# Half-height last products for neighbouring first layer tiles of a gated MLP behind a recurrent attention

## The chip, the cores and the metric

The kernel runs on one core of one Trainium2 chip. The metric is the device time of one execution in microseconds; three executions of the kernel before took 619.6, 621.16 and 621.56 us, so the median is 621.16 us.

## What is computed

The first half is a recurrence over 768 time steps for 4 x 8 heads with a 40 x 40 state, whose output is laid out as `x` of shape 4 x 768 x 320. The second half, which the change touches, is a gated MLP on `x`:

```python
def _moe_ref(x, w_in, g_ln, w_sg, b_sg, w_out):
    h = x @ w_in                        # 320 -> 1024
    h = gelu(h)                         # tanh form
    u, v = h[..., :512], h[..., 512:]
    v_n = layernorm(v) * g_ln           # over the 512
    v_s = einsum('ts,bsd->btd', w_sg, v_n) + b_sg    # over the 768 time steps
    return x + (u * v_s) @ w_out        # 512 -> 320
```

All inputs are float32, and the result has to be near float32: each factor of a product is split into a high and a low part that TensorE's one-pass type (float32r) holds, and a product is taken as high x high + high x low + low x high.

## The kernel before

The recurrence is done by chunks of 64 steps, with all of its products in plain float32. Its last chunks overlap with the first pieces of the MLP; from about 375 us on the MLP is alone. The MLP works on one batch at a time, in pieces whose order is written out in the lists `SEQ0` (batch 0, with the first tiles of batch 1), `SEQ` (batches 1 and 2, each with the tiles of the next) and `SEQL` (batch 3). Each piece is one method of `Mlp`:

- `x0`, `x1` (`split_x`): split 384 time steps of `x` into high `xh` and low `xl`, one ScalarE copy and one VectorE subtraction per block of 128 rows. `x` has 320 rows: two blocks of 128 and one of 64. The third block of `xh` holds the 64 rows twice: the high part in partitions 0 to 63, the low part in 64 to 127. The third block of the weights (`wih`, `wil`) holds the same 64 rows of `w_in` in both halves.
- `v0` to `v5` (`in_v`): 128 time steps by 512 columns of the first layer's `v` half; `u0` to `u7` (`in_u`): 128 columns by 384 time steps of its `u` half. These are the first layer tiles. Each takes eight products into one PSUM bank: `xh` by `wih` (three blocks), `xh` by `wil` (three blocks), `xl` by `wih` (two blocks).
- `s0` to `s7` (`sgu`): 18 products of the spatial layer, from the split `v` tiles and the split spatial weights `wsh`, `wsl`; `o0` to `o5` (`outp`): the second layer, twelve products, or eight for the last 64 rows, which alternate between 64 and 128 columns.

`product` issues a piece's matmuls and hands its later steps to `later`, each with a lag in pieces and a rank; `tick`, called once per piece, issues the steps that are due, in order of rank, and that is the order in which ScalarE, VectorE and GpSimd run them. For a tile these are: lag 0, Square on ScalarE (tile `p`) and the first VectorE step (`q`); lag 1, Tanh on ScalarE (in place in `q`) and the VectorE step that reads the PSUM bank last (into `u` or `v`); for a `v` tile also the norm's statistics (`bs`, `mv`, `rs`), a GpSimd power on `rs`, and with lag 2 the normalisation and the split into `vh` (ScalarE) and `vl` (GpSimd). Every engine runs its instructions in program order. PSUM has eight banks in a ring, one for each piece that multiplies.

Loads and weight splits are `jobs` in `run`, issued ahead of the piece whose place in the sequence they name. The tiles x0, v0, v1, v2, u0 of batch 0 (`FILL`) are issued while the recurrence still runs. `EARLY` is the number of `v` pairs (`vh`, `vl`, 4 KB per partition each pair) that lie in the pool that opens early; the rest lie in the pool that opens after the recurrence.

In the profile nearly all instructions carry line 157, that of the helper that records them, so the rows are read by tiles: `hv` and `hu` are the PSUM tiles of v and u, `sg` and `op` those of the spatial and the second layer, `ab`, `ut`, `pq`, `yp`, `ru` and `sp` belong to the recurrence, `idle` are products without use.

Of the kernel before, what the change touches and what calls it, by code (L numbers as in the profile page):

```python
# [9 lines left out]
F32 = mybir.dt.float32  # L10
F32R = mybir.dt.float32r
I32 = mybir.dt.int32
AF = mybir.ActivationFunctionType
ALU = mybir.AluOpType
PSUM = bass.MemoryType.PSUM

B, H, S, D = 4, 8, 768, 40
# [65 lines left out]
FILL = (("x0", 0, 319.86), ("v0", 0, 331.35), ("v1", 0, 344.98), ("v2", 0, 346.14), ("u0", 0, 349.9))  # L83
AFTER = {"v": (0.56, 0.57, 1.47, 1.57, 2.13, 2.48, 2.96, 4.17, 5.19), "u": (1.14, 1.97, 2.82, 3.17), "x": ()}
PX1 = 0
EARLY = 4
PSG = 313.1
SGD = (-6.74, -0.32, 1.37)
SGA = ()
VRING = 10  # L90
SEQ = ("x0", "s1", "x1", "s2", "s0", "s3", "s4", "v0", "s5", "v1", "o0", "o1", "o2", "s6", "s7", "v2", "u0", "v3",
    "u1", "v4", "v5", "o3", "o5", "o4", "u2", "u3", "u4", "u5", "u7", "u6")
SEQ0 = (("x0", 0), ("v0", 0), ("v1", 0), ("v2", 0), ("u0", 0), ("u3", 0), ("x1", 0), ("u1", 0), ("u2", 0), ("v3",
# [8 lines left out]
XE = "VVVVVVVVVVVV"  # L102
# [23 lines left out]
class Banks:  # L126


    def __init__(self, tc, ctx):
        self.tc, self.ctx, self.n = tc, ctx, 0  # L130
        self.rings = [ctx.enter_context(tc.tile_pool(name="ps", bufs=6, space=PSUM))] * 6
# [30 lines left out]
def engines(tc):  # L162
    nc = tc.nc
    return tuple(InOrder(tc, e) for e in (nc.vector, nc.scalar, nc.gpsimd, nc.tensor, nc.sync))
# [720 lines left out]
class Mlp:  # L885
# [3 lines left out]
    def __init__(self, tc, ps, xd, w_in, w2, g_ln, wst, b_sg, w_out, out):  # L889
        self.tc, self.ps, self.xd, self.out = tc, ps, xd, out  # L890
        self.w_in, self.w2, self.g_ln, self.wst, self.b_sg, self.w_out = w_in, w2, g_ln, wst, b_sg, w_out
        self.V, self.A, self.G, self.T, self.Q = engines(tc)
        self.ctx = ExitStack()
        self.vn, self.us, self.gs, self.xin, self.left, self.outs = {}, {}, {}, {}, [8] * B, {}
        self.ready = set()
        self.n, self.todo, self.plan, self.hold, self.held = 0, [], None, None, {}

    def pool(self, nm, side):
        return self.ctx.enter_context(self.tc.tile_pool(name=nm, bufs=1, side=side, reuse_waits="tile"))
# [8 lines left out]
    def open_x(self):  # L908
        p = self.pool("mlp_x", "right")
        self.xts = {(0, 0): self.xtile(p, 0, 0)}  # L910
        self.xh = p.tile([128, 3, S], F32R, name="xh")
        self.xl = p.tile([128, 2, S], F32R, name="xl")

    def xtile(self, p, b, n):
        return p.tile([128, 3, S // 2], F32, name=f"xt{b}{n}")

    def open_v(self):
        self.pv = p = self.pool("mlp_v", "right")
        self.xts.update({x: self.xtile(p, *x) for x in ((1, 0), (0, 1))})
        self.free = self.pairs(p, 0, EARLY)  # L920
        self.ut = {(f, 0): p.tile([128, 384], F32, name=f"u{f}") for f in range(4)}
# [27 lines left out]
    def open_rest(self):  # L949
# [5 lines left out]
        self.xts[1, 1] = self.xtile(p, 1, 1)  # L955
        self.free += self.pairs(p, EARLY, VRING)
        self.ut.update({(f, 1): p.tile([128, 384], F32, name=f"u{4 + f}") for f in range(4)})
# [126 lines left out]
    def split_x(self, b, n):  # L1084
        t, h, l = self.xts[b % 2, n], self.xh, self.xl
        self.xin[n] = b
        c = slice(384 * n, 384 * n + 384)
        for k in range(2):
            self.split(h[:, k, c], l[:, k, c], t[:, k], self.A, self.pick(XE, 6 * b + 3 * n + k))
        self.A.copy(out=h[:, 2, c], in_=t[:, 2])  # L1090
        self.pick(XE, 6 * b + 3 * n + 2).tensor_tensor(out=h[64:128, 2, c], in0=t[64:128, 2], in1=h[64:128, 2, c].bitcast(F32), op=ALU.subtract)

    def pick(self, s, k):
        return self.G if k < len(s) and s[k] == "G" else self.V

    def product(self, ops, *steps):
        for i, (o, l, r) in enumerate(ops):
            self.T.matmul(o, lhsT=l, rhs=r, start=(i == 0), stop=(i == len(ops) - 1), skip_group_check=True)
        if self.hold is not None:
            self.hold += [f for _, _, f in sorted(steps, key=lambda x: x[:2])]  # L1100
            return
        self.later(*steps)
        self.tick()
# [10 lines left out]
    def in_v(self, b, tt):  # L1114
        V, G, sb = self.V, self.G, self.pv
        xh, xl, wih, wil = self.xh, self.xl, self.wih, self.wil
        c, f = slice(128 * tt, 128 * tt + 128), slice(HF, DF)
        ops = [(xh[:, k, c], x[:, k, f]) for x in (wih, wil) for k in range(3)]
        ops += [(xl[:, k, c], wih[:, k, f]) for k in (0, 1)]
        o, v = self.ps("hv"), sb.tile([128, HF], F32, name="v", bufs=3)  # L1120
        mv = sb.tile([128, 2], F32, name="mv", bufs=3)
        rs = sb.tile([128, 1], F32, name="rs", bufs=3)
        bs = sb.tile([128, 6], F32, name="bs", bufs=3)
        pair = self.free.pop(0)
        assert self.xin[tt // 3] == b

        def root():
            V.tensor_scalar(out=rs, in0=mv[:, 1:2], scalar1=4e-6, scalar2=None, op0=ALU.add)
            G.tensor_tensor(out=rs, in0=rs, in1=self.mhalf, op=ALU.pow)

        def halves():
            h, l = pair
            self.split(h, l, v)
            self.vn[b, tt] = h, l

        self.product([(o, *x) for x in ops], *self.gelu2(o, HF, v),
                     (1, 7, lambda: V.bn_stats(out=bs, in_=v)), (1, 8, lambda: V.bn_aggr(out=mv, in_=bs)), (1, 9, root),
                     (2, 7.5, lambda: V.tensor_scalar(out=v, in0=v, scalar1=mv[:, 0:1], scalar2=rs,
                                                    op0=ALU.subtract, op1=ALU.mult)),
                     (2, 10, halves))  # L1140

    def in_u(self, b, f, n):
        xh, xl, wih, wil = self.xh, self.xl, self.wih, self.wil
        fc, c = slice(128 * f, 128 * f + 128), slice(384 * n, 384 * n + 384)
        ops = [(x[:, k, fc], xh[:, k, c]) for x in (wih, wil) for k in range(3)]
        ops += [(wih[:, k, fc], xl[:, k, c]) for k in range(2)]
        o = self.ps("hu")[:, 0:384]
        assert self.xin[n] == b
        u = self.us[b, f, n] = self.ut.pop((f, n))
        self.product([(o, *x) for x in ops], *self.gelu2(o, 384, u))  # L1150

    def sgu(self, b, f, n):
        V, sb = self.V, self.pr
# [127 lines left out]
    def run(self, ahead, verdict=None):  # L1281

        done = [(x, b) for x, b, _ in FILL] if ahead else []
        seq, jobs = [], []
        if not ahead:
            self.ps.grow()
            self.open_in()
            for g in self.weights_in():
                for f in g(self.G):
                    f()  # L1290
            self.open_x()
            self.open_v()
            self.open_sg()
        self.open_rest()
        for b in range(B):
            seq += [(x, b + (x[0] in "uvx")) for x in (SEQL if b == B - 1 else SEQ)] if b else list(SEQ0)
        seq = [x for x in seq if x[1] < B and x not in done and (ahead or x[0][0] != "j")]
        for i, (x, b) in enumerate(seq):
            if x[0] == "x" and (b or not ahead) and not (ahead and (x, b) == ("x0", 1) and PX1):
                jobs.append((max(0, i - XL), lambda b=b, n=int(x[1]): self.load_x(b, n)))  # L1300
            if verdict and (x, b) == ("s7", 1):
                jobs.append((i, lambda: self.later((8, 9, verdict()))))
        rest, loads, parts, wo = self.weights_rest([(i % 6, i // 6) for i, _ in SGA] if ahead else [])
        jobs += [(REST - 3, rest[0]), (REST, rest[1])]
        for k, f in enumerate(loads):
            if f:
                jobs.append((SGS[k - 5] if k > 4 else 0, f))
        for k, f in enumerate(parts):
            if f:
                jobs.append((SGS[k], f))  # L1310
        for k, g in enumerate(wo):
            for d, f in zip(OSTEP, g):
                jobs.append((OUTS[k] + d, f))
        jobs.sort(key=lambda x: x[0])
        for i, (x, b) in enumerate(seq):
            while jobs and jobs[0][0] <= i:
                jobs.pop(0)[1]()
            self.piece(x, b)
        self.flush()
        self.ctx.close()  # L1320
# [111 lines left out]
```

## Time and profile before

| | before |
|---|---|
| median of three runs | 621.16 us |
| the profiled execution's own time | 620.27 us |
| span of the profiled execution | 618.5 us |
| mean granted TensorE clock | 0.945 |
| TensorE busy | 578.4 us, 94% |
| VectorE busy | 487.2 us, 79% |
| ScalarE busy | 390.9 us, 63% |
| GpSimd busy | 374.3 us, 61% |

Busy time is the time in which an engine has at least one instruction running; loads of TensorE's stationary operand are counted apart (PEld). The ends of products are modelled, and successive products overlap in the record: the time a product takes in a stream is the distance between starts. Span is from the first to the last instruction; the execution's own time has a little more around it.

### The profile page before, as it was taken

To read this page: it belongs to the slowest core of one execution; us is meant where nothing else is said; L and a number is where in the kernel's file an instruction comes from. 1 tells how busy PE (TensorE), PEld (TensorE's weight loads), DVE (VectorE), ACT (ScalarE), POOL (GpSimd) and SP (SyncE) were. 2 spreads that over 40 slices of the span, in tenths; PEclk is the share of its full clock that TensorE was granted. 3 is DMA by queue.
4 is the path that set the end of the run, shared out by engine and by line. 5 is a ranking of instruction groups with operands and counts; after the bars stand their busy time and mean duration, and the time that the engine had idled before them with its cause. 6 is when DMAs were issued, how large, how long until landed. Compare 5 with 4: busy or idle time off the path is not lost.

```text
span 618.5 us, 24511 instructions
## 1 busy us (share of the span) xinstructions
PE 578.4 (94%) x10060; PEld 520.8 (84%) x10060; DVE 487.2 (79%) x1085; ACT 390.9 (63%) x1113; POOL 374.3 (61%) x842
## 2 busy tenths in 40 slices
PE   5758999999999999999979999699999999999996
PEld 5557888888888888888868789699899989999995
DVE  7867798988889897798787988898887779568732
ACT  6938798988979889788764856544544256224410
POOL 7768688888888888888886425445533332343230
PEclk9555899999999999999989999899999999999999
DMA  6513243454434543433433424420111103010002
GB/s 207 168 41 89 76 123 104 121 129 117 113 106 117 132 120 104 116 100 92 140 92 100 129 78 141 141 65 10 33 55 54 34 1 108 1 34 13 20 1 70
DMA packets 56889, 54.06 MB, mean 87 GB/s; under 512 B 35840, under 2 KB 47360, under 8 KB 56768
## 3 DMA queue, kind: packets, MB, share of 16 engines
q1 hardware_dynamic: 56768, 52.40, 29.9%
q8 instruction: 81, 1.33, 0.9%
q14 instruction: 40, 0.33, 0.2%
HBM read 44.52 MB, written 7.86 MB: 85 GB/s over the span
## 4 chain that ended last, share of the span: by engine, by line
PE 50%; DVE 15%; ACT 14%; POOL 9%; issue 6%; DMA 4%; SPq 1%; POOLq 0%; ACTq 0%; DVEq 0%
PE sg L157 13%; PE op L157 6%; PE hu L157 6%; PE hv L157 6%; POOL x L157 5%; POOL tg L157 4%; PE ab L157 4%; ACT nts L157 3%; PE sp L157 3%; PE yp L157 3%; PE ru L157 2%; DVE at L157 2%; DMA main<-main 2%; DVE sc L157 2%; DVE ex L157 2%
## 5 line engine op out<-in xcount | busy, mean ns | idle before, releaser
L157 POOL TENSOR_TENSOR tg<-x,n 128x126 f32<-128x126 f32 (+24 forms) x334 | 123.1, 369 | 34.2 <-ACT x L157 5.5
L157 POOL TENSOR_TENSOR x<-x,tg 128x126 f32<-128x126 f32 (+24 forms) x334 | 126.3, 378 | 26.1
L157 PE MATMUL sg<-wsh,vh 128*128 128x384 f32 x192 | 66.0, 344 | 5.7 <-ACT wsh L157 4.5
L157 POOL TENSOR_TENSOR gx<-g,gy 128x384 fp32r<-128x384 f32 x30 | 31.7, 1061 | 64.6 <-ACT gy L157 64.6
L157 PE MATMUL sg<-wsl,vh 128*128 128x384 f32 x192 | 65.7, 342 | 0.4 <-POOL wsl L157 0.4
L157 PE MATMUL sg<-wsh,vl 128*128 128x384 f32 x192 | 65.7, 342 | 0.0
L157 ACT ACTIVATE nts<-ab 32x256 f32<-32x256 f32 x192 | 62.0, 323 | 5.7 <-DVE at L157 3.1
L157 PE MATMUL pq<-rt,vut 128*64 128x128 f32 x768 | 52.9, 281 | 0.0
L157 ACT CAST gy<-g 128x384 fp32r<-128x384 f32 x30 | 15.4, 514 | 55.5 <-DVE g L157 52.2
L157 PE MATMUL ab<-at,kb 64*64 64x64 f32 x1536 | 38.5, 242 | 11.0 <-POOL kb L157 5.4
L157 ACT CAST vh<-v 128x512 fp32r<-128x512 f32 x24 | 14.9, 621 | 51.6 <-DVE v L157 51.6
L157 PE MATMUL yp<-pqs,kbt 128*64 128x64 f32 x768 | 46.5, 225 | 1.0 <-ACT kbt L157 0.4
L157 PEld LDWEIGHTS ab<-at,kb 64*64 64x64 f32 x1536 | 31.7, 150 | 16.6 <-POOL kb L157 6.0
L157 POOL TENSOR_TENSOR vl<-v,vh 128x512 fp32r<-128x512 f32 x24 | 31.6, 1317 | 20.9 <-ACT vh L157 20.9
L157 PEld LDWEIGHTS pq<-rt,vut 128*64 128x64 f32 x768 | 41.8, 139 | 2.3 <-issue 0.7
L157 PEld LDWEIGHTS sg<-wsh,vh 128*128 128x128 f32 x192 | 36.9, 192 | 6.6 <-ACT wsh L157 4.8
L157 PE MATMUL yp<-rt,s 80*40 80x64 f32 x704 | 42.3, 219 | 0.0
L157 PEld LDWEIGHTS yp<-pqs,kbt 128*64 128x64 f32 x768 | 37.1, 136 | 5.4 <-DVE sc L157 2.2
L157 DVE SCALAR_TENSOR_TENSOR g<-sg,gl,bt 128x384 f32<-128x384 f32 x32 | 19.7, 615 | 25.4 <-PE sg L157 24.4
L157 DVE TENSOR_TENSOR at<-ab,mask 64x256 f32<-64x256 f32 x96 | 35.7, 407 | 4.5 <-PE ab L157 3.9
L157 PEld LDWEIGHTS sg<-wsl,vh 128*128 128x128 f32 x192 | 36.9, 192 | 1.0 <-POOL wsl L157 0.8
L157 PE MATMUL ru<-rhsb,xt 64*64 64x40 f32 x768 | 32.2, 234 | 5.7 <-ACT xt L157 5.3
(166 smaller groups left out, 1652.7 us busy)
## 6 DMA issues: line engine op xcount, KB each, us to landing
main<-main SPq DMA_DIRECT2D x88, 160.8 KB
vs<-vb SPq DMA_DIRECT2D x24, 160.0 KB
vu<-vs SPq DMA_DIRECT2D x24, 160.0 KB
rt<-rt SPq DMA_DIRECT2D x48, 80.0 KB
vut<-vt SPq DMA_DIRECT2D x24, 160.0 KB
xd<-yt SPq DMA_DIRECT2D x96, 40.0 KB
xt<-xd SPq DMA_DIRECT2D x16, 192.0 KB
out<-y SPq DMA_DIRECT2D x16, 192.0 KB
```

The source lines that it names most:

```text
L157: return self.tc.keep_in_program_order(f(*a, **k))
```

## The change

Three things are changed. In the x split, the high part of the third block is also written to the upper partitions of a new tile `xb`, and the low part is made from that. In a pair of neighbouring first layer tiles, the product of `wil`'s third block (which only needs 64 rows: the high part of `x`) is left out of each tile's list, and after the second tile's products two products of 64 rows are issued, one for each tile: the first tile's with partitions 0 to 63 (from `xh`), the second's with 64 to 127 (from `xb`), each into its own tile's bank. The first tile's later steps are handed on only then. A tile without a neighbour keeps its product of 128 rows. `run` forms the pairs from left to right in the sequence. Besides, `SEQ` has `v1` ahead of `s5`, and `EARLY` is 3.

```diff
-EARLY = 4
+EARLY = 3
-SEQ = ("x0", "s1", "x1", "s2", "s0", "s3", "s4", "v0", "s5", "v1", "o0", ...
+SEQ = ("x0", "s1", "x1", "s2", "s0", "s3", "s4", "v0", "v1", "s5", "o0", ...
...
+        self.xb = p.tile([128, S], F32R, name="xb")
...
-        self.A.copy(out=h[:, 2, c], in_=t[:, 2])
-        self.pick(XE, 6 * b + 3 * n + 2).tensor_tensor(out=h[64:128, 2, c], in0=t[64:128, 2], in1=h[64:128, 2, c].bitcast(F32), op=ALU.subtract)
+        z = self.xb[64:128, c]
+        self.A.copy(out=z, in_=t[64:128, 2])
+        self.A.copy(out=h[0:64, 2, c], in_=t[0:64, 2])
+        self.pick(XE, 6 * b + 3 * n + 2).tensor_tensor(out=h[64:128, 2, c], in0=t[64:128, 2], in1=z.bitcast(F32), op=ALU.subtract)
...
-    def product(self, ops, *steps):
-        for i, (o, l, r) in enumerate(ops):
-            self.T.matmul(o, lhsT=l, rhs=r, start=(i == 0), stop=(i == len(ops) - 1), skip_group_check=True)
+    def product(self, ops, *steps, third=None):
+        ops = [(*x, not i, i == len(ops) - 1 and not third) for i, x in enumerate(ops)]
+        if third and not self.pair:
+            ops.append((*third(slice(0, 128)), False, True))
+        if third and self.pair == 2:
+            for k, f in enumerate((self.first[0], third)):
+                ops.append((*f(slice(64 * k, 64 * k + 64)), False, True))
+        for o, l, r, start, stop in ops:
+            self.T.matmul(o, lhsT=l, rhs=r, start=start, stop=stop, skip_group_check=True)
+        if third and self.pair == 1:
+            self.first = third, steps
+            return
+        if third and self.pair == 2:
+            self.later(*self.first[1])
+            self.tick()
...
# in_v (in_u alike, with weights and x in each other's place)
-        ops = [(xh[:, k, c], x[:, k, f]) for x in (wih, wil) for k in range(3)]
+        ops = [(xh[:, k, c], x[:, k, f]) for x in (wih, wil) for k in range(3 if x is wih else 2)]
+        def third(r):
+            return o, (self.xb[r, c] if r.start else xh[r, 2, c]), wil[r, 2, f]
...
# run, for each piece
+            if self.pair == 1:
+                self.pair = 2
+            else:
+                self.pair = int(x[0] in "uv" and i + 1 < len(seq) and seq[i + 1][0][0] in "uv")
             self.piece(x, b)
```

## Rows read from the trace of the kernel before

**Rows 1.** Busy us (and count) by engine in two stretches, clock, DMA share, GB/s.

```profile
382.00:434.70 52.70, 46.62 (x237) 43.60 (x235) 45.72 (x106) 26.40 (x66) 25.70 (x35) 0.94 0.26 78
434.70:612.90 178.20, 178.09 (x980) 171.32 (x980) 124.85 (x250) 66.93 (x135) 59.90 (x62) 1.00 0.11 35
```

**Rows 2.** Chain of waits: 382.0 to 434.7 by line, then pieces (start, us, what).

```profile
by line: DVE sc L157 13.1%; DVE g L157 11.6%; issue 9.0%; DVE lt L157 6.0%; DVE v L157 5.6%; DVE stg L157 5.4%; DVE q L157 4.7%; DMA xt<-xd 4.4%; DVE wsl L157 4.1%; ACT wsh L157 4.1%; SPq L157 4.0%; ACT p L157 3.8%; DVE bs L157 2.7%; DVE xl
...
493.65 1.81 PE hv L157 x8
495.46 1.41 PE hu L157 x8
...
612.86 0.56 DVE y L157
```

**Rows 3.** TensorE's waits, 350 to 618.5: total us, times, longest.

```profile
PE sg L157 <- ACT wsh L157: 4.5, 1, 4.5
PE sg L157 <- DVE v L157: 1.2, 1, 1.2
```

**Rows 4.** TensorE in order of time, into 64 rows: start, us, what.

```profile
359.83 0.39 PE L157 MATMUL hv<-wih,xl 128*128 128x512 f32 x1
360.15 0.25 PE L157 MATMUL ut<-ident,vu 64*80 64x64 f32 x1
```

**Rows 5.** TensorE in order of time: out of halves, first full products, an ordinary one.

```profile
360.52 0.27 PE L157 MATMUL ut<-ident,vu 64*80 64x64 f32 x2
360.72 0.27 PE L157 MATMUL yp<-pqs,kbt 128*64 128x64 f32 x1
...
358.12 0.50 PE L157 MATMUL hv<-wih,xh 128*128 128x512 f32 x1
...
372.69 0.34 PE L157 MATMUL hu<-xl,wih 128*128 128x384 f32 x1
...
374.02 0.45 PE L157 MATMUL hu<-xh,wih 128*128 128x384 f32 x1
```

**Rows 6.** TensorE in order of time: four quarters, and one row half.

```profile
203.43 0.69 PE L157 MATMUL ab<-at,kb 64*64 64x64 f32 x32
...
360.15 0.64 PE L157 MATMUL ut<-ident,vu 64*80 64x64 f32 x8
```

**Rows 7.** TensorE in order of time: second layer, 64 and 128 columns.

```profile
446.47 0.51 PE L157 MATMUL op<-gx,woh 128*64 128x384 f32 x2
446.81 0.33 PE L157 MATMUL op<-gy,woh 128*128 128x384 f32 x1
446.99 0.33 PE L157 MATMUL op<-gx,woh 128*64 128x384 f32 x1
```

**Rows 8.** ScalarE in order of time, 380 to 390, with idle before.

```profile
380.43 0.60 ACT L157 ACTIVATE p<-hv 128x512 f32<-128x512 f32 x1
...
382.25 0.60 ACT L157 ACTIVATE p<-hv 128x512 f32<-128x512 f32 x1 [0.41 <-PE hv L157]
...
387.70 0.62 ACT L157 CAST vh<-v 128x512 fp32r<-128x512 f32 x1 [2.52 <-DVE v L157]
```

**Rows 9.** VectorE in order of time, 381 to 389.

```profile
382.88 0.69 DVE L157 SCALAR_TENSOR_TENSOR q<-p,hv 128x512 f32<-128x512 f32 x1 [0.67 <-ACT p L157]
383.48 0.68 DVE L157 SCALAR_TENSOR_TENSOR v<-q,hv 128x512 f32<-128x512 f32 x1
...
387.13 0.53 DVE L157 TENSOR_SCALAR v<-v,mv,rs 128x512 f32<-128x512 f32 x1
```

**Rows 10.** TensorE in order of time: the first spatial product that waits.

```profile
397.53 0.69 PE L157 MATMUL sg<-wsh,vh 128*128 128x384 f32 x1 [4.52 <-ACT wsh L157]
```

**Rows 11.** ScalarE and VectorE around an x split.

```profile
408.67 1.32 ACT L157 CAST xh<-xt 128x384 fp32r<-128x384 f32 x3
...
411.81 1.03 DVE L157 TENSOR_TENSOR wsl<-ws,wsh 128x384 fp32r<-128x384 f32 x2
```

**Rows 12.** TensorE: a u tile's first product behind a bank.

```profile
457.53 0.41 PE L157 MATMUL hu<-xh,wih 128*128 128x384 f32 x1
```

More of the change, by code (lines that the diff above doesn't have):

```diff
@@ L90 @@
 VRING = 10
-SEQ = ("x0", "s1", "x1", "s2", "s0", "s3", "s4", "v0", "s5", "v1", "o0", "o1", "o2", "s6", "s7", "v2", "u0", "v3",
+SEQ = ("x0", "s1", "x1", "s2", "s0", "s3", "s4", "v0", "v1", "s5", "o0", "o1", "o2", "s6", "s7", "v2", "u0", "v3",
     "u1", "v4", "v5", "o3", "o5", "o4", "u2", "u3", "u4", "u5", "u7", "u6")
@@ L896, in __init__ @@
         self.n, self.todo, self.plan, self.hold, self.held = 0, [], None, None, {}
+        self.pair, self.first = 0, None
     def pool(self, nm, side):
@@ L1139, in in_v @@
                                                     op0=ALU.subtract, op1=ALU.mult)),
-                     (2, 10, halves))
+                     (2, 10, halves), third=third)
     def in_u(self, b, f, n):
@@ L1144, in in_u @@
         fc, c = slice(128 * f, 128 * f + 128), slice(384 * n, 384 * n + 384)
-        ops = [(x[:, k, fc], xh[:, k, c]) for x in (wih, wil) for k in range(3)]
+        ops = [(x[:, k, fc], xh[:, k, c]) for x in (wih, wil) for k in range(3 if x is wih else 2)]
         ops += [(wih[:, k, fc], xl[:, k, c]) for k in range(2)]
@@ L1149, in in_u, with third @@
         u = self.us[b, f, n] = self.ut.pop((f, n))
-        self.product([(o, *x) for x in ops], *self.gelu2(o, 384, u))
+        def third(r):
+            return o, wil[r, 2, fc], (self.xb[r, c] if r.start else xh[r, 2, c])
+        self.product([(o, *x) for x in ops], *self.gelu2(o, 384, u), third=third)
     def sgu(self, b, f, n):
```

## The prediction

> **What bounds the kernel now.** I read the busy time by stretches first, then the chain of waits in order of time, then TensorE's own waits, and last the order of single products where TensorE changes from one tile geometry to another. The stretches divide the second half of the span in two. From 434.7 to 612.9 us TensorE is busy for 178.09 of 178.20 us at a granted clock of 1.00 (the level of 2.4 GHz) while VectorE has 124.85 [rows 1], and the chain there is nothing but products until the last addition at 612.86 [rows 2]: a product more or less is time more or less. From 382.0 to 434.7 TensorE has 46.62 of 52.70 us [rows 1] and the chain runs through VectorE and ScalarE, weight splitting above all [rows 2]; TensorE's two long waits, 4.5 us for a split spatial weight and 1.2 us for a PSUM bank, are both there [rows 3]. So the change must be priced twice: by products after 434.7, by the order on VectorE and ScalarE before it.
>
> **How many pairs.** By the lists SEQ0 and SEQ (with v0 and v1 now neighbours) 23 pairs form: 4 in batch 0, 5 in batch 1, 7 each in batches 2 and 3. By the kinds of the two tiles 10 are u-u (384 columns), 6 v-v (512 columns), 7 mixed. Five (all of batch 0, and v2-u0 of batch 1) lie before 434.7; 18 lie in the TensorE-bound stretch: 8 u-u, 5 v-v, 5 mixed.
>
> **What a pair takes away.** Eight products of a v tile take 1.81 us and eight of a u tile 1.41 [rows 2], 0.227 and 0.176 each. A pair has 16 full products now; afterwards 14, and two with 64 rows. If those two run beside each other, one product is gone.
>
> That two row halves can run beside each other the trace shows: 32 records of `ab`, spread over four quarters of the array, take 0.69 us from the first start to the last end, against 0.64 for the eight of `ut`, which stand in one row half one after the other [rows 6]. There the second half starts into another PSUM bank, as it will here. I take the concurrency as given, with about 0.007 us between the two starts.
>
> **What a pair adds on TensorE.** The trace has no 64-row product of this data type (float32r), so I take the nearest rows.
> - Into the halves: the last full product of `hv` starts at 359.83, the first `ut` (64 rows) at 360.15 [rows 4]. Full `hv` products follow each other at 0.227; so 0.32 - 0.227 = 0.09 us is lost before the first half starts.
> - Out of them: the last two `ut` start at 360.52 and, at their pace of 0.056, 360.58; the next geometry starts at 360.72 [rows 5]: 0.14 - 0.056 = 0.09 us again.
> - Weights: in a steady stream the load of the next stationary operand is hidden. The first full product after a change of geometry is longer by it: 0.50 instead of 0.39 us for `hv` [rows 4, 5], 0.45 instead of 0.34 for `hu` [rows 5], 0.11 each. This is for 128 columns, and the 64-row halves have 128 columns too. I price 0.11 on the way in (both halves loading together, as the quarters of `ab` do) and 0.11 on the way out.
>
> Together 0.09 + 0.11 + 0.09 + 0.11 + 0.007 = 0.41 us. Against it stands the product saved: 0.176 where the pair has a u tile, 0.227 for v-v. A pair with a u tile costs 0.41 - 0.176 = 0.23 us, a v-v pair 0.41 - 0.227 = 0.18. In the bound stretch: 13 x 0.23 + 5 x 0.18 = 3.9 us more. From the other side: if nothing is lost at the change, 18 pairs save 13 x 0.17 + 5 x 0.22 = 3.3 us; if the halves run one after another besides the loss, they add about 18 x 0.4 = 7.4.
>
> A row speaks for the low end. `op` goes back and forth between 128 and 64 columns, and its products start at 446.47, 446.64, 446.81 and 446.99, 0.17 apart [rows 7]: nothing is lost there, and these are float32r. But they always start at column 0 and use all 128 rows; each change of row count that I found loses the 0.09. I take the loss.
>
> The Trainium skill (TensorEngine Tiling (Array Packing), section Tiling Modes, under Key Properties) says that a change of tiling mode, not just of tile, drains the array. The rows of `ut` agree, with 0.09 us each way; it gives no price, and no word of the weight load behind it. TensorE: Matmul & The Clock Gate (section Part 3: Packing small matmuls) has a pack last one product plus about 4 ns per tile; by that alone each pair would save a product, which is the first rival below.
>
> **What moves.** The first tile's steps are now issued after the second tile's products. VectorE, ScalarE and GpSimd get the same steps in the same order (only the weight jobs of a pair's second position come ahead of the first's steps), but Square of the first tile now waits about one tile longer, and everything behind it on ScalarE waits too. Where those engines are already behind TensorE that is nothing, and for the u tiles of batch 0 behind v5 they are. It matters at one place, v3-v4 of batch 0. Square of v3 runs at 380.43 and that of v4, waiting for TensorE, at 382.25 [rows 8]. Afterwards both can start only at 382.25 plus what the two pairs up to there add (0.23 for u1-u2, about nothing for v3-v4 before its end), say 382.45. Then VectorE takes q of v3 at 383.1, the u of the tile before (0.6), q of v4 (0.6), and reaches v of v3 at 384.75 where it now starts at 383.48 [rows 9]: 1.2 us late. From there the chain has no slack: normalisation at 387.13 [rows 9], its cast at 387.70 on ScalarE [rows 8], and behind them in order the Squares of u4, u6, u5, u7 and the cast of the weight for which the first spatial product waits 4.52 us, until 397.53 [rows 10]. VectorE is then the bound to 434.7. So +1.2 us, with 0 (absorbed) and 2 as bounds.
>
> The extra ScalarE copy of each x split (8 times 0.41, a third of 1.32 in [rows 11]) is hidden: at 376 by the wait for the pair, at 408.7 because VectorE reads the weights cast behind it only at 411.81 [rows 11], later because ScalarE has 66.93 us of work in 178.2 [rows 1]. Uncovered it would be 3.3 us. The fourth v pair's move into the later pool (EARLY) costs nothing: its tile is first written at 387.70 [rows 8], when the attention is over; the pool's other tiles shift by 4 KB, which can move loads by 0 to 1 us either way. PSUM banks are held one tile longer. The tightest bank is that of a u tile at 457.53, whose first product has 0.41 us instead of 0.34 [rows 12]; VectorE's part of that race is late by 1.2 us, TensorE's by 1.2 and what three pairs add, so no new wait. After it TensorE has no wait at all [rows 3], so I expect none there.
>
> **Sum.** 3.9 + 1.2 = +5.1 us on a profiled execution of 620.27 us (span 618.5). The median of the three runs, 621.16, lies 0.9 above it: 626.3 us. Own range of this case 624.5 to 627.8.
>
> **Rivals.**
> 1. No loss at the change: float32r halves follow full products as the 64 columns of `op` do [rows 7]. Then each pair gives back its product. Up to 457.5 the bank holds TensorE back anyway [rows 12], so 15 pairs count: 11 x 0.17 + 4 x 0.22 = 2.7 us; the v3 delay shrinks to 0.6. Sum -2.1: 619.1 us. It decides once loss and loads together stay under about 0.15 us a pair; the changes in the trace show 0.4 [rows 4, 5]. Chance 0.12.
> 2. It doesn't do what it says: the halves run one after another in the full geometry, as `op` at 64 columns, without loss or gain. TensorE is as before, the delay of about 1.0 stays: 622.2 us. For it: the `op` rows; against it: `ab`. Chance 0.14.
> 3. Loss and no concurrency: each pair adds another product, perhaps also a load: 18 x 0.2 to 18 x 0.3 more, 629.9 to 631.7 us. Against it stand the 32 `ab` in 0.69 us [rows 6]. Chance 0.11.
> 4. The forecast but for its smaller part: loads partly hidden, or the v3 delay absorbed: 623.0 to 624.5. Chance 0.10. The forecast itself: 0.53.
>
> **Numbers.** A measurement of this kernel tells a change of about 0.3% (1.9 us) from none. Faster than that (under 619.3) is half of rival 1 and a little for wrong side effects: 0.10. Within it are rival 2, the rest of rival 1 and some of case 4: 0.22. Slower: 0.68. The range for 8 in 10 leaves out rival 1 and most of rival 3: 621.5 to 630.0.
>
> **What would show it.** Right: in the trace afterwards each pair's two 64-row products start some 0.01 us apart, the first about 0.32 (behind 512 columns) or 0.27 (behind 384) after the last full one, the first full product after them has 0.50 or 0.45 us instead of 0.39 or 0.34, and TensorE's products per pair last 0.2 us longer; the spatial product that now starts at 397.53 starts over 1 us later. Wrong: halves that start at the stream's pace (rival 1), or 0.17 to 0.23 apart (rivals 2 and 3); or a wait of TensorE for a PSUM bank after 460, which I have at none.

## The result, and the profile after

| | before | after |
|---|---|---|
| median of the runs beside each other | 621.36 us (4 runs, 619.6 to 621.72) | 625.48 us (4 runs, 624.69 to 626.31) |
| profiled execution, own time | 620.27 us | 624.69 us |
| its span | 618.5 us | 623.0 us |
| mean granted TensorE clock | 0.945 | 0.955 |
| TensorE, VectorE, ScalarE, GpSimd busy | 578.4, 487.2, 390.9, 374.3 us | 579.0, 491.2, 395.6, 373.2 us |

After over before is 1.0079, with a 95% interval of 1.0058 to 1.0101: slower by 4.9 us on 621, with 626.3 us forecast and 621.5 to 630.0 as range.

The recurrence ahead of the MLP doesn't take the same time in each execution: the first product of tile u3 of batch 0 starts at 374.02 us in the trace of before, at 373.37 in that of after, and anywhere from 372.6 to 375.5 in the others below. From there on the stretches of one kernel repeat (in two traces of before: 60.71 and 60.73 us, 177.75 and 177.72). So I compare stretches that begin and end at a named product. A is from u3's first product to the first product of `s7` of batch 0, the last product of TensorE that waits; B is from there to the last product of the second layer. After takes 62.36 us in A (1.65 more than before) and 181.30 in B (3.55 more): +5.20 us in all.

Busy us (and count) by engine in the two windows of the trace of after that answer to [rows 1], with clock, DMA share and GB/s:

```profile
382.00:435.70 53.70, 46.47 (x236) 41.70 (x234) 46.89 (x107) 28.18 (x70) 25.09 (x35) 0.94 0.26 76
435.70:617.40 181.70, 181.64 (x980) 166.99 (x980) 127.61 (x249) 69.63 (x139) 59.45 (x62) 1.00 0.11 34
```

Behind 435.7 TensorE is busy all the time, as it was, at the same clock, and the window is 3.5 us longer with the same 980 records. (Each pair has two half products in place of two full ones. That two of them run at once can't be seen in a busy time; it must be read from starts.) Two v tiles with the second layer behind them, and then two u tiles (TensorE's products in after, in order of time: start, us, what; the profile writes f32 for float32r products too):

```profile
505.27 0.39 PE L157 MATMUL hv<-wih,xl 128*128 128x512 f32 x1
505.59 0.50 PE L157 MATMUL hv<-wil,xh 64*128 64x512 f32 x1
505.59 0.50 PE L157 MATMUL hv<-wil,xb 64*128 64x512 f32 x1
506.02 0.45 PE L157 MATMUL op<-gy,woh 128*128 128x384 f32 x1
506.30 0.34 PE L157 MATMUL op<-gy,wol 128*128 128x384 f32 x1
...
517.12 0.51 PE L157 MATMUL hu<-xl,wih 128*128 128x384 f32 x2
517.56 0.44 PE L157 MATMUL hu<-xh,wil 64*128 64x384 f32 x1
517.56 0.44 PE L157 MATMUL hu<-xb,wil 64*128 64x384 f32 x1
517.93 0.79 PE L157 MATMUL hu<-xh,wih 128*128 128x384 f32 x3
518.55 0.51 PE L157 MATMUL hu<-xh,wil 128*128 128x384 f32 x2
```

The second line of a pair starts with the first; in the unrounded records it is 3 or 4 ns behind, at all 23 pairs. In the u pair the last full product (the second of the x2) starts at 517.29, so the halves come 0.27 later where the stream has 0.17. The next full product is 0.37 behind the halves, not 0.17, and itself takes 0.28: the three products of 517.93 last until 518.55, which is 0.62 = 0.28 + 2 x 0.17. In the v pair the same distances are 0.32, 0.43 and 0.28. That answers to [rows 4, 5]: the change of geometry in, a weight load, the change out, a weight load. The loads can be seen by themselves (TensorE's loads of the stationary operand in after, around the same u pair):

```profile
517.12 0.19 PEld L157 LDWEIGHTS hu<-xl,wih 128*128 128x128 f32 x1
517.55 0.18 PEld L157 LDWEIGHTS hu<-xh,wil 64*128 64x128 f32 x1 [0.25 <-issue]
517.56 0.18 PEld L157 LDWEIGHTS hu<-xb,wil 64*128 64x128 f32 x1
517.93 0.19 PEld L157 LDWEIGHTS hu<-xh,wih 128*128 128x128 f32 x1 [0.18 <-issue]
```

The load of 517.12 is for the product of 517.29: one product ahead. Those of 517.55, 517.56 and 517.93 start together with the product that uses them. Across a change of geometry the load didn't run ahead. A product whose load starts with it takes 0.10 to 0.11 us longer here, and just as much behind a wait without any change of geometry (groups of six, below: three products in 512.46 - 511.83 = 0.63 = 0.28 + 2 x 0.17). So I put the 0.11 down to the load, though the record of the load itself is 0.18 us long.

TensorE's waits from 350 us on (total, times, longest), which answer to [rows 3]:

```profile
PE sg L157 <- ACT wsh L157: 5.2, 1, 5.2
PE hv L157 <- DVE xh L157: 0.9, 1, 0.9
PE sg L157 <- DVE v L157: 0.7, 1, 0.7
PE sg L157 <- POOL wsl L157: 0.4, 1, 0.4
```

All four lie in A. The first is 0.7 us longer, the wait of `s7` for VectorE (the third line) 0.5 shorter, and the second is not in the first trace of before. None is in B.

### The profile page after: what moved, and what is told of

It is laid out like the page before. It is cut to its first block, busy times and chain, and to the rows that moved or that the text cites. A ratio compares the mean times of both kernels' runs of the same rounds, so it can differ in the third digit from the quotient of the medians.

```text
span 623.0 us, 24519 instructions
## 1 busy us (share of the span) xinstructions
PE 579.0 (93%) x10060; PEld 511.3 (82%) x10060; DVE 491.2 (79%) x1085; ACT 395.6 (64%) x1121; POOL 373.2 (60%) x842
## 4 chain that ended last, share of the span: by engine, by line
PE 45%; DVE 19%; ACT 16%; POOL 8%; issue 7%; DMA 3%; SPq 0%; DVEq 0%; POOLq 0%; ACTq 0%
PE sg L157 13%; PE op L157 6%; PE hv L157 6%; PE hu L157 6%; ACT nts L157 4%; POOL x L157 4%; POOL tg L157 4%; DVE at L157 3%; PE yp L157 3%; DVE ex L157 3%; DVE fixed L157 2%; ACT junk L157 2%; PE ab L157 2%; PE sp L157 2%; PE gp L157 2%
## 5 line engine op out<-in xcount | busy, mean ns | idle before, releaser
L157 POOL TENSOR_TENSOR rs<-rs,mhalf 128x1 f32<-128x1 f32 x24 | 13.7, 570 | 50.3 <-DVE rs L157 44.7
```

The source lines that it names most:

```text
L157: return self.tc.keep_in_program_order(f(*a, **k))
```

## The experiments

The stretches of all kernels, in us, each worked out from the starts of the named products in its trace; "sum" is A + B against before, "as ratio" that sum over 621.4 us, to be held against the measured ratio of the runs (it is not the quotient of the medians, and can differ from it by some 0.2%). The second column ends at the spatial product of [rows 10], the first that waits for a weight.

| kernel | u3 to the product of [rows 10] | A | B | sum | as ratio | measured (95%) |
|---|---|---|---|---|---|---|
| before | 23.50 | 60.71 | 177.75 | | | |
| before, again | 23.50 | 60.73 | 177.72 | -0.01 | | |
| after | 25.03 | 62.36 | 181.30 | +5.20 | 1.0084 | 1.0079 (1.0058 to 1.0101) |
| order alone | 24.53 | 61.74 | 177.73 | +1.01 | 1.0016 | 1.0018 (0.9999 to 1.0037) |
| no pairs | 23.50 | 60.80 | 177.56 | -0.10 | 0.9998 | 0.9998 (0.9978 to 1.0019) |
| same rows | 25.42 | 62.42 | 184.67 | +8.63 | 1.0139 | 1.0150 (1.0116 to 1.0183) |
| no pairs in batch 0 | 23.50 | 60.76 | 181.30 | +3.60 | 1.0058 | 1.0051 (1.0026 to 1.0076) |
| three pairs per change | 23.50 | 60.80 | 177.40 | -0.26 | 0.9996 | 1.0000 (0.9973 to 1.0027) |
| each half alone | 24.88 | 62.19 | 191.88 | +15.61 | 1.0251 | 1.0232 (1.0196 to 1.0268) |
| groups of six | 23.50 | 60.53 | 186.41 | +8.48 | 1.0136 | 1.0122 (1.0081 to 1.0164) |

Every ratio of a trace lies inside the interval of the runs, so the runs don't contradict the stretches. These intervals reach 1 to 3 us to each side; that a stretch can be read finer rests on the two traces of before, which agree to 0.03 us. Each kernel is the changed one with the edit shown. The absolute times expected were worked out from a before of 621.4 us; in the runs beside the first four experiments before has 622.25, beside the others 621.69.

**The order without the halves.** Both products keep 128 rows; the steps of a pair's first tile stay delayed.

```diff
-                ops.append((*f(slice(64 * k, 64 * k + 64)), False, True))
+                ops.append((*f(slice(0, 128)), False, True))
```

> The two products at a pair's end use all 128 rows again, so no geometry changes and none is saved; only the later issue of the first tile's steps (and the extra copy, pools, SEQ) is left. My theory (about 3.5 to 3.9 us of the loss are changes of geometry, 1.0 to 1.5 us the order before the spatial products of batch 0): 622.4 to 622.9 us against 621.4 before; TensorE's stretch from the last wait to the end as before (183.8 us in the profile). Rival (the later steps are the cause, in all batches): 625 us, as with the change.

Measured: 622.94 us (12 runs) against 622.25. B is that of before (177.73 against 177.75), so the delay of steps costs nothing that shows where TensorE is the bound. (It is 0.17 more than without pairs, below: the bank of [rows 12] comes free 22.8 us behind the start of `s7` in both, and here one product fewer stands ahead of it.) A is 1.03 us longer, and the product of [rows 10] comes 24.53 us after u3, not 23.50 (TensorE in order of time):

```profile
399.81 0.69 PE L157 MATMUL sg<-wsh,vh 128*128 128x384 f32 x1 [5.53 <-ACT wsh L157]
```

The wait there is 1.0 us longer than the 4.52 of [rows 10], without any change of geometry in the kernel. The order term is in the trace, and it is in A; the runs alone (0.9999 to 1.0037) don't tell it from none.

**No pairs.** What is left is the x split with its third copy, the order of `SEQ` and `EARLY`.

```diff
-                self.pair = int(x[0] in "uv" and i + 1 < len(seq) and seq[i + 1][0][0] in "uv")
+                self.pair = 0
```

> No pairs are formed: each tile has its eight products of 128 rows and its steps as before; left are the extra ScalarE copy of each x split, EARLY 3 and v1 ahead of s5. My theory: these are hidden, 621.4 us within 0.5. Rival (the fourth ScalarE copy or the pools shifted by 4 KB are part of the loss): 622 to 624 us.

Measured: 621.75 us (12 runs) against 622.25, no difference; A +0.09, B -0.19. The copies and the pool cost nothing that can be measured. Against this kernel the 18 pairs of B cost 181.30 - 177.56 = 3.74 us.

**Both halves in the same rows.** The second tile's half uses partitions 0 to 63 too, so that the two can't run beside each other; the work and the changes of geometry are the same.

```diff
-                ops.append((*f(slice(64 * k, 64 * k + 64)), False, True))
+                ops.append((*f(slice(0, 64)), False, True))
...
-            return o, (self.xb[r, c] if r.start else xh[r, 2, c]), wil[r, 2, f]
+            return o, (xh[r, 2, c]), wil[r, 2, f]
```

> Both 64-row products of a pair use rows 0 to 63, so they cannot run beside each other; two changes of geometry per pair as with the change. My theory (with the change they do run together): the second starts a product later, 0.17 or 0.23 us, so 18 pairs add 3.3 us, up to 5.3 if its load is bare too: 628.8 to 630.8 us. Rival (they ran one after another with the change already): 625.5 us, the same as the change.

Measured: 630.9 us (6 runs) against 622.25, and B is 3.37 us longer than in after. That is one more half per pair, 13 x 0.174 + 5 x 0.227 = 3.40, and no second load. A pair of u tiles (TensorE in order of time):

```profile
523.99 0.44 PE L157 MATMUL hu<-xh,wil 64*128 64x384 f32 x1
524.27 0.34 PE L157 MATMUL hu<-xh,wil 64*128 64x384 f32 x1
524.54 0.44 PE L157 MATMUL sg<-wsh,vh 128*128 128x384 f32 x1
```

Now the halves are 0.28 apart, which is the stream's 0.17 and the 0.11 of the load that opens the geometry, and the full product follows 0.27 behind: 0.17 and the change out. So with the change as made the halves do run beside each other.

**No pairs in batch 0.**

```diff
-                self.pair = int(x[0] in "uv" and i + 1 < len(seq) and seq[i + 1][0][0] in "uv")
+                self.pair = int(b > 0 and x[0] in "uv" and i + 1 < len(seq) and seq[i + 1][0][0] in "uv")
```

> The four pairs of batch 0 are undone, the other 19 stay. My theory (v3's Square a tile later delays the first spatial products, and VectorE carries it to about 435 us): 1.0 to 1.5 us less than the change, 624.0 to 624.5, and the first spatial product that waits for its weight is back at about 397.5. Rival (TensorE's time alone counts, and batch 0 lies where it is not the bound): 625.5, as with the change.

Measured: 625.5 us (12 runs) against 622.25. The absolute figures named there are missed, and by number it is the rival's 625.5: on this chip before has 622.25, not the 621.36 from which I worked, and the change itself would come to 627.2 by its ratio of 1.0079. And u3 starts at 375.48, not 374.02, so that the product of [rows 10] starts late and yet waits as before:

```profile
398.98 0.69 PE L157 MATMUL sg<-wsh,vh 128*128 128x384 f32 x1 [4.52 <-ACT wsh L157]
```

In the stretches it is as expected: 23.50 us behind u3, A 60.76, B that of after to 0.01 us. The ratio falls from 1.0079 to 1.0051; those intervals overlap, so by medians alone this step is not shown, by the traces it is.

**Three pairs per change of geometry.** Only where six u tiles stand in a row, their six halves are collected and issued as three pairs behind the last of them; all other tiles keep 128 rows. (The roles of the tiles are found ahead of `run`'s loop: 1 for the first five, 2 for the sixth, 0 for the rest.)

```diff
-            for k, f in enumerate((self.first[0], third)):
-                ops.append((*f(slice(64 * k, 64 * k + 64)), False, True))
+            for k, f in enumerate((*(x for x, _ in self.first), third)):
+                r = 64 * (k % 2)
+                ops.append((*f(slice(r, r + 64)), False, True))
...
```

> Only the six u tiles in a row of batches 2 and 3 are grouped: 42 full products, then six of 64 rows in three pairs behind one change into halves and one out; no other tile is paired. My theory (a fixed 0.40 us per change in and out with its two bare loads, and a product of 0.174 saved per pair): each group 0.41 + 0.01 - 0.52 = -0.10 us; the stretches between the first spatial products of batches 1, 2 and 3 take 58.76 and 58.37 us (before 58.86 and 58.47), and the time is that of before within the noise. Within a group the pairs start about 0.17 apart after the first. Rival (each pair of halves pays a bare load or a stall anew): the pairs start 0.28 or more apart and each group costs 0.1 us or more. Rival (holding six banks makes TensorE wait): some us in these stretches, with a wait for a bank in the rows.

Measured: 620.65 us (10 runs) against 621.69, ratio 1.0000 (0.9973 to 1.0027): no loss any more, and no gain that the runs can tell. One group (TensorE in order of time; the second product of the first line starts at 516.24):

```profile
516.06 0.51 PE L157 MATMUL hu<-xl,wih 128*128 128x384 f32 x2
516.50 0.44 PE L157 MATMUL hu<-xh,wil 64*128 64x384 f32 x1
516.51 0.44 PE L157 MATMUL hu<-xb,wil 64*128 64x384 f32 x1
516.78 0.33 PE L157 MATMUL hu<-xh,wil 64*128 64x384 f32 x1
516.79 0.33 PE L157 MATMUL hu<-xb,wil 64*128 64x384 f32 x1
516.96 0.34 PE L157 MATMUL hu<-xh,wil 64*128 64x384 f32 x1
516.96 0.34 PE L157 MATMUL hu<-xb,wil 64*128 64x384 f32 x1
517.23 0.45 PE L157 MATMUL sg<-wsh,vh 128*128 128x384 f32 x1
517.51 0.34 PE L157 MATMUL sg<-wsl,vh 128*128 128x384 f32 x1
```

In 0.27, then 0.28 from the first pair to the second, 0.17 to the third, out 0.27, and 0.28 for the first full product. The losses are there once, not three times: 516.24 to 517.51 is 1.27 us where eight full products would take 8 x 0.174 = 1.39, so a group of three gains 0.12 while a single pair loses 0.23. B is 0.16 us shorter than without pairs, with two groups in it, where two gains of 0.12 make 0.24. The stretches forecast at 58.76 and 58.37 us took 58.56 and 58.24 (58.78 and 58.34 without pairs); of the 0.22 by which the first is the shorter, 0.11 is only the bare load of the spatial product behind the group, which falls into the next stretch. The remaining 0.08 I have not traced. No wait for a bank shows in B, though the groups hold six.

**Each half alone.** A tile's half is issued with its own tile, one change of geometry for each, and no step is delayed.

```diff
-        if third and self.pair == 2:
-            for k, f in enumerate((self.first[0], third)):
-                ops.append((*f(slice(64 * k, 64 * k + 64)), False, True))
+        if third:
+            r = {0: slice(0, 128), 1: slice(0, 64), 2: slice(64, 128)}[self.pair]
+            ops.append((*third(r), False, True))
...
-        if third and self.pair == 1:
-            self.first = third, steps
-            return
-        if third and self.pair == 2:
-            self.later(*self.first[1])
-            self.tick()
```

> The same 46 tiles have a 64-row last product, the first of a pair in rows 0 to 63, the second in 64 to 127, but each right behind its own seven, so that the array changes geometry twice as often and nothing runs beside anything; the steps are as before. My theory: each tile loses 0.40 us and saves nothing, 36 tiles from the last wait to the end make 14.5 us there (177.75 before, 192.2 here), and the time is 636 to 637 us. Rival (what a pair loses with the change is mostly that its two halves disturb each other, not the changes of geometry): well under that, 625 to 630 us.

Measured: 636.12 us (4 runs) against 621.69; B is 14.13 us longer than before. A single half (TensorE in order of time):

```profile
522.07 0.51 PE L157 MATMUL hu<-xl,wih 128*128 128x384 f32 x2
522.51 0.44 PE L157 MATMUL hu<-xb,wil 64*128 64x384 f32 x1
522.88 0.79 PE L157 MATMUL hu<-xh,wih 128*128 128x384 f32 x3
```

From the last full product (522.24) to the half 0.27, to the next full one 0.37, and 0.28 for that one: 0.92 us instead of 3 x 0.174 = 0.52, a loss of 0.40. That is the price of going in and coming out with nothing saved against it, measured by itself; 36 halves in B make 36 x 0.40 = 14.4. A is 1.48 us longer too, though no step is delayed: ahead of the product of [rows 10] the time of the changes comes through.

**Groups of six of either kind.** As three pairs per change, but runs of six neighbouring tiles of u or v (v2 u0 v3 u1 v4 v5) form groups too, four groups in all (edit against three pairs per change).

```diff
-            while i + n < len(seq) and seq[i + n][0][0] == "u":
+            while i + n < len(seq) and seq[i + n][0][0] in "uv":
```

> As the run with three pairs per change, and the six tiles v2 u0 v3 u1 v4 v5 of batches 2 and 3 are a group too. My theory of fixed cost: those groups give 0.41 - 0.17 - 0.17 - 0.23 = -0.16 us each, so the stretches of batches 2 and 3 lose 0.26 us each against before, unless the late steps of four v tiles at once cost TensorE a wait. Rival: VectorE needs some 2.6 us for each v tile, starts them 8 us later, and a wait for a bank or for the last v tile's split takes 1 to 4 us per batch.

Measured: 630.37 us (4 runs) against 621.69. By products alone it should be faster than the kernel with two groups (a group of the new kind takes 1.49 us from its last full product to the second one behind it, where full products would take 1.66); it is 8.48 us longer in A + B than before. So the theory failed and the rival held, with more than the 1 to 4 us per batch that it was given (5.4 in batch 2 and 3.3 in batch 3, between the first spatial products and against no pairs). TensorE waits again (total, times, longest; 350 us to the end):

```profile
PE hu L157 <- DVE v L157: 3.5, 4, 1.4
PE hu L157 <- DVE u L157: 1.4, 2, 0.7
...
PE op L157 <- DVE u L157: 0.7, 1, 0.7
```

These are banks: the VectorE step that writes `v` or `u` is the one that reads a tile's bank last, and the waits behind the first such group end, in order, with the steps of u0, v3, u1 and v4. And busy time by engine, clock, DMA share and GB/s behind one of those groups:

```profile
508.00:512.00 4.00, 2.92 (x17) 2.32 (x16) 2.89 (x6) 2.43 (x5) 1.85 (x2) 1.00 0.01 4
512.00:516.00 4.00, 2.82 (x14) 2.17 (x14) 2.75 (x7) 1.54 (x3) 1.39 (x2) 1.00 0.00 0
516.00:520.00 4.00, 3.05 (x10) 2.69 (x11) 3.86 (x9) 0.73 (x2) 0.99 (x2) 0.66 0.14 49
520.00:524.00 4.00, 4.00 (x24) 3.75 (x24) 3.40 (x9) 1.24 (x2) 2.28 (x3) 0.91 0.11 25
```

Six tiles hold six of the eight banks until the group ends, and all their steps come behind it. Six u tiles do so without a wait, as three pairs per change shows; here four of the six are v tiles, each with its norm. VectorE isn't full in the first two windows (2.89 and 2.75 of 4 us); ScalarE, in program order, stands still for 2.51 us ahead of each cast of a `v` tile until VectorE has normalised it, and the next tile's Square comes behind that cast (ScalarE, then one of TensorE's waits, in order of time):

```profile
509.53 0.62 ACT L157 CAST vh<-v 128x512 fp32r<-128x512 f32 x1 [2.51 <-DVE v L157]
510.05 0.49 ACT L157 ACTIVATE p<-hu 128x384 f32<-128x384 f32 x1
...
511.83 0.79 PE L157 MATMUL hu<-xh,wih 128*128 128x384 f32 x3 [0.35 <-DVE v L157]
512.46 0.51 PE L157 MATMUL hu<-xh,wil 128*128 128x384 f32 x2
```

TensorE misses 3.2 us here (1.1, 1.2 and 0.9 in three windows), and in the third of these windows the granted clock is 0.66 in the mean, so for part of it at 1.2 instead of 2.4 GHz. So what the groups save in changes of geometry is paid for in banks. No version beat the kernel before.

**The kernel before, once more,** for its stretches in a second trace:

> The kernel before once more, for its stretches: from the tile u3 of batch 0 to the last wait 60.7 us and from there to the last product of the second layer 177.75 us, within 0.2; what comes ahead of u3 may differ by 1 to 2 us between runs.

Measured: 620.89 us in one run; the stretches are in the table.

## Why the prediction was right

Forecast and measurement, term by term:

| step of the prediction | forecast | measured |
|---|---|---|
| change in, per pair | 0.09 us | 0.094 (0.268 - 0.174; 0.319 - 0.227) |
| load on the way in, change out | 0.11 + 0.09 | 0.20 (0.37 - 0.17), together |
| load on the way out | 0.11 | 0.105 to 0.11 |
| between the two starts | 0.007 | 0.003 to 0.004 |
| net, pair with a u tile | +0.23 | +0.22 to +0.23 |
| net, v-v pair | +0.18 | +0.17 to +0.18 |
| 18 pairs of the bound stretch | +3.9 | +3.74 against the kernel without pairs |
| order ahead of 434.7 | +1.2 | +1.65, of which 1.03 in order alone |
| sum | +5.1 | +5.20 in the stretches |

- **The pairs.** All five terms held, though the changes in and out were taken from plain float32 products of the recurrence [rows 4, 5] and applied to float32r. Of the two rows that disagreed, the row halves spoke for this change and `op` [rows 7] did not: `op` changes columns and keeps its 128 rows. The experiments show each of the terms by itself: concurrency by the same rows (+3.37), the price of the change by each half alone (0.40 each), and that it is paid per change and not per pair by three pairs per change. The Trainium skill (TensorEngine Tiling (Array Packing), section Tiling Modes, under Key Properties) has the array drain at a change of tiling mode; the runs agree in that each change by itself loses 0.09 us, and show that two of the four losses are of another kind, loads that start with their own product instead of ahead of it.
- **The order.** The mechanism held; ScalarE and VectorE in after, in order of time, show it against [rows 8, 9]:

```profile
381.78 0.60 ACT L157 ACTIVATE p<-hv 128x512 f32<-128x512 f32 x1 [1.31 <-PE hv L157]
...
382.68 0.59 ACT L157 ACTIVATE p<-hv 128x512 f32<-128x512 f32 x1
...
388.39 0.62 ACT L157 CAST vh<-v 128x512 fp32r<-128x512 f32 x1 [2.00 <-DVE v L157]
```

```profile
384.07 0.68 DVE L157 SCALAR_TENSOR_TENSOR v<-q,hv 128x512 f32<-128x512 f32 x1
...
387.83 0.53 DVE L157 TENSOR_SCALAR v<-v,mv,rs 128x512 f32<-128x512 f32 x1
```

Square of v3 now waits for v4's products and the two Squares stand 0.9 us apart (1.82 in [rows 8]); v of v3 comes at 384.07, with u3 0.65 us earlier than in before, so 384.07 - 383.48 + 0.65 = 1.24 us late: 1.2 was forecast. But behind it the delay grew to 1.5 us at the product of [rows 10]:

```profile
398.41 0.69 PE L157 MATMUL sg<-wsh,vh 128*128 128x384 f32 x1 [5.17 <-ACT wsh L157]
...
412.84 0.47 PE L157 MATMUL hv<-wih,xh 128*128 128x512 f32 x1 [0.93 <-DVE xh L157]
```

398.41 - 397.53 + 0.65 = 1.53. The order alone gives 1.03 there; the other 0.5 is changes of geometry, which I had counted as hidden in batch 0 but for the first pair's. The trace of the order alone, where u3 starts at 375.28, tells the parts apart (ScalarE, VectorE, in order of time):

```profile
383.28 0.60 ACT L157 ACTIVATE p<-hv 128x512 f32<-128x512 f32 x1 [1.01 <-PE hv L157]
...
385.58 0.68 DVE L157 SCALAR_TENSOR_TENSOR v<-q,hv 128x512 f32<-128x512 f32 x1
```

From u3, Square of v3 starts at 8.00 us there and at 8.41 in after, both times right behind TensorE, and v of v3 is 0.84 and 1.24 us late: the 0.4 between them is what the pairs u1-u2 and v3-v4 add on TensorE. Square of v5 comes right behind TensorE too and brings 0.1 more with v5's own pair, so that the normalisation of v3 is 1.35 late (0.84 with the order alone). The last 0.2 is in both kernels: the normalisation ahead of the third cast takes 0.73 us, and 0.54 in before. So the 1.24 that met the forecast was 0.84 of order, for which I had about 1.0, and 0.4 of geometry, for which I had 0.2: that it met it is luck. The whole term was 0.45 us too small.
- **No new wait.** In the bound stretch there is none, as forecast. In A there is one, the second line above: a v tile waits 0.9 us for the third block of the x split. The added copy is not shown to be its cause: in the second trace of before, which hasn't the copy, the wait is 0.3 us, and in the order alone, which has it, there is none (0.5 without pairs). Nor does it show in the time: `s7` still waits 0.7 us for VectorE behind it, and from the product of [rows 10] to `s7` it is 37.20 us in before, 37.22 in the order alone and 37.33 in after.
- **What cancelled.** The order term was 0.45 too small, and the pairs, against the kernel before itself, 0.35 too large (3.55 in B for 3.9; 0.19 of it is the gain of the kernel without pairs). The profiled executions differ by 4.4 us and not 5.2, because the recurrence of the one of after ended 0.65 us earlier; the medians by 4.1, the ratio of the runs makes 4.9. So the sum's 0.1 us of error is in part luck: two errors of 0.35 and 0.45 us stand against each other.
- **The rivals.** Rival 1 (no loss) falls with the distances in every pair, 0.27 or 0.32 us in and 0.37 or 0.43 out; rival 2 (no effect) and rival 3 (no concurrency) with the 4 ns between the halves, and the latter's 629.9 to 631.7 us is where the kernel with both halves in the same rows came out, 630.9. Rival 4 (the forecast's smaller part) falls with 3.55 us in B and 1.65 in A: neither was hidden.

## What to carry to other kernels

Using half of the array's rows twice at once saves one product per pair, but each visit to another geometry cost 0.40 us here (0.09 in, 0.09 out, and a bare 0.11 us load behind each), more than two products of 384 columns. So collect three pairs of 384 columns or more behind one change, or leave it; even three gave only 0.12 us a group in the trace, and nothing that the runs could tell. Count then what the collecting holds: six u tiles held six banks without a wait, but with four v tiles among the six the steps behind the group came too late for the banks, and that cost more than the changes had. And a step that is issued later cost nothing where TensorE was the bound, but 1.03 us where the engines that run it had no slack, so ask it stage by stage.

## What the runs showed that I had not expected

- Two 64-row products in one geometry, in the same rows, hide the second's load: 0.28 us apart right behind the change, of which 0.11 is the first's own load. In three pairs per change the second pair comes 0.28 and the third 0.17 behind. The bare load goes with the change of geometry, not with the 64 rows; it is also there behind a wait for a bank.
- The two halves of a pair start 3 to 4 ns apart, at 384 and at 512 columns.
- The kernel without pairs (two v tiles ahead of `s5`, the copy, the pools) is 0.19 us faster in B than before. It was costed at nothing, and which of the three does it I did not separate.
- The row halves go on by themselves. In a group v2 u0 v3 u1 v4 v5 the half of u1 stands behind that of v3 in the program and starts 0.05 us before it, 0.28 us behind the half of u0 in the same rows (TensorE in groups of six; u1 is the second product of the first line, in the unrounded records at 503.89):

```profile
503.61 0.61 PE L157 MATMUL hu<-xb,wil 64*128 64x384 f32 x2
503.94 0.39 PE L157 MATMUL hv<-wil,xh 64*128 64x512 f32 x1
```

- In groups of six a run of waits, in which TensorE was busy for 2.92, 2.82 and 3.05 of 4 us each, came with a granted clock of 0.66 in the last 4 us and 0.91 in the next, so the waits cost more than their own length. Behind the same group of batch 3 TensorE was busy for 3.71, 2.98 and 2.76 of 4 us and the clock stayed at 1.00.
